# Grouped-query decode attention: a loop of two blocks run 15 times, with K in three 32 KB pieces

## The chip, the core and the metric

One core of a Trainium2 chip runs the whole kernel. The time is device microseconds of one execution, as the median of three runs; beside it one execution was profiled, and its trace is what the views below come from. The engines are PE (matrix multiply, with its weight loads shown as PEld), DVE (vector), ACT (scalar functions), POOL (GpSimd) and SP, which here only issues DMAs. Every large load is issued by SP and runs on 16 DMA engines.

## What is computed

A decode step of attention for one token, mixed with a small token mixer by a gate:

```python
q = (x @ wq)                       # 16 heads of 256
scores = einsum("bhqd,bhkd->bhqk", q, k) * (256 ** -0.5)   # k: 8 kv heads x 65536 keys x 256
p = softmax(scores)
a = einsum("bhqk,bhkd->bhqd", p, v).reshape(1, 1, 16 * 256) @ wo
h = layernorm(x); u = gelu(einsum("bsd,sf->bdf", h, w1) + b1); b = einsum("bdf,fs->bds", u, w2) + b2
g = sigmoid((x * gate_w).sum(-1))
out = g * a + (1 - g) * b
```

x has 448 elements; K and V are 268 MB each in bf16. Two query heads share one K/V head.

## The kernel before

The keys are cut into 32 blocks of 16,384: four per K/V head. A block's K and V are 8.39 MB each. Partition p of a tile holds 128 consecutive keys, so a full K or V block is 64 KB per partition, and half of it 32 KB.

SBUF holds one K block in two tiles of 32 KB per partition (`k_tiles[0]`, `k_tiles[1]`, shown as kn), one V block in one tile of 64 KB (`vt`), two tiles `kT` for transposed K, and the whole output projection `wo_sb` (28 KB per partition).

A block runs through `block` (L537), whose order is the order on each engine, since `seq` ties every instruction to the one before it on its engine:

- `score_block` (L381): eight steps; in each DVE transposes 16 keys per partition (L365) into one of the two kT tiles, and PE makes 8 matmuls into the score tile (L373). The first four steps read the first K tile, the last four the second.
- the loads, issued by SP: `load_v` of this block (L130), then the two halves of the next block's K (L124). V waits until the P·V of the block before has read vt; each K half waits for the four transposes that read its tile.
- `softmax` (L425): a maximum on DVE (L431), a transpose on PE (L435), the running maximum, the exponential on ACT (L452), a transpose of the weights on DVE (L460). Blocks after the first of a head rescale the running sums; the first one overwrites them. In a head's last block DVE copies the next head's q (`place_q`, L303).
- `products`: 64 matmuls of P·V (L393), then DVE adds them to the running sum (L470, L475).
- in a head's last block `denominators` and `head_end` (L508): normalise, collect, project with Wo (L503), add to `a_acc` (L514).

Ahead of that stand the q projection, the layer norm, and 14 gelu activations on ACT (L263) whose results lie in wo_sb until Wo is loaded. Block 0 is peeled off: it has the gate's sum, the mixer's 14 matmuls and tail as hooks between its steps, and issues the load of 14 heads of Wo (3.2 MB).

The loop (L556) runs 7 times over four blocks, with a `tc.stage_boundary()` between blocks; with `iteration_sync="staggered"` the loop body is cut into four stages, and each engine has semaphore instructions at each boundary and at the back edge. Three blocks follow it. The last block's V goes into the two K tiles in eight pieces, which P·V and `columns` take up one by one.

Of the kernel before, what the change touches and what calls it, by code (L numbers as in the profile page):

```python
# [14 lines left out]
HQ = 16  # L15
# [11 lines left out]
QW = 128 + 2 * NI  # L27


@with_exitstack  # L30
def kernel(
# [48 lines left out]
    kvpool.tile([128, 4096 - 128], mybir.dt.uint8, name="fill")  # L80
    k_tiles = [kvpool.tile([128, KP, DH], BF16, name=f"kn{i}") for i in range(2)]
# [4 lines left out]
    wo_sb = const.tile([128, HQ, 2, D], BF16)  # L86
# [5 lines left out]
    f_tiles = [psum.tile([64, MC], FP32, name=f"f{i}") for i in range(2)]  # L92
    f_rows = [f_tiles[k][32 * k:32 * k + 1, :] for k in range(2)]
# [13 lines left out]
    gel = wo_sb[:].rearrange("p h c n -> p (h c) n")[:, 0:NF, :]  # L107

    def place(n):
        return n if isinstance(n, tuple) else divmod(n, NB)  # L110

    def following(n):
        g, b = place(n)
        return (g + (b + 1) // NB, (b + 1) % NB)

    def rows(cache, n):
        g, b = place(n)
        return cache[0, bass.ds(g, 1), b * BLK:(b + 1) * BLK, :].rearrange(
            "o (p j) d -> (o p) j d", j=VP
        )  # L120

    def load_k(n, h, pieces=((0, KP),)):
        for j0, j1 in pieces:
            seq(nc.sync.dma_start(  # L124
                out=k_tiles[h][:, j0:j1, :],
                in_=rows(A_k_cache, n)[:, h * KP + j0:h * KP + j1, :],
            ))

    def load_v(n, j0=0, j1=VP):
        seq(nc.sync.dma_start(out=vt[:, j0:j1, :], in_=rows(A_v_cache, n)[:, j0:j1, :]))  # L130
# [3 lines left out]

    LAST = ((0, 32), (32, 64), (64, 80), (80, 96), (96, 112), (112, 120), (120, 124), (124, 128))

    def load_wo(h0, h1):
        seq(nc.sync.dma_start(
            out=wo_sb[:, h0:h1],
            in_=A_wo[h0 * DH:h1 * DH, :].rearrange("(h p c) n -> p h c n", p=128, c=2),  # L140
        ))

    def load_v_last(n):
        for j0, j1 in LAST:
            seq(nc.sync.dma_start(
                out=k_tiles[j0 // KP][:, j0 % KP:(j1 - 1) % KP + 1, :],
                in_=rows(A_v_cache, n)[:, j0:j1, :],
            ))
# [12 lines left out]
    load_k(0, 0, ((0, 32), (32, KP)))  # L161
    load_k(0, 1)
# [74 lines left out]
    xf = work.tile([128, D], FP32)  # L237
    h_bc = work.tile([128, D], FP32)
    w1f = const.tile([128, NF], FP32)
    b1f = const.tile([128, NF], FP32)  # L240
    seq(nc.vector.tensor_copy(out=xf[:], in_=sm_ps[:, 0:D]))
    seq(nc.vector.bn_stats(out=stats[:], in_=xf[:]))
# [8 lines left out]
    for _ in range(2):  # L251
# [7 lines left out]
        out=h_bc[:], in0=xf[:], scalar1=mv[:, 0:1], scalar2=rstd[:, 0:1],  # L259
        op0=ALU.subtract, op1=ALU.mult,  # L260
    ))
    for b in range(NF):
        seq(nc.scalar.activation(  # L263
            out=gel[:, b, :], in_=h_bc[:], func=ACT.Gelu_apprx_tanh,
            scale=w1f[:, b:b + 1], bias=b1f[:, b:b + 1],
        ))
# [30 lines left out]
    qq = const.tile([128, 2 * NW, HQ], BF16)  # L297
    seq(nc.vector.tensor_copy(out=qq[:], in_=qq_ps.rearrange("p (w h) -> p w h", h=HQ)))

    def place_q(g):  # L300
        for a in range(NQ):
            quad = slice(32 * a, 32 * (a + 1))
            seq(nc.vector.tensor_copy(  # L303
                out=qz[quad, :, 2 * NI + 32 * a:2 * NI + 32 * a + REP],
                in_=qq[quad, :, bass.ds(g * REP, REP)],
            ))

    place_q(0)
    zt = work.tile([1, D], FP32)
# [7 lines left out]
    def gate_sum():  # L317
        seq(nc.vector.tensor_tensor(out=zt[:], in0=xf[0:1, :], in1=gw[:], op=ALU.mult))
        seq(nc.vector.tensor_reduce(out=z[:], in_=zt[:], op=ALU.add, axis=AXIS.X))
        seq(nc.scalar.activation(out=ez[:], in_=z[:], func=ACT.Exp, scale=-1.0))  # L320

    def mixer_tail():
# [4 lines left out]
        y_ps = hd_ps[0:1, 0:D]  # L327
        for b in range(NF):
            seq(nc.tensor.matmul(
                y_ps, lhsT=w2b[:, b:b + 1], rhs=gel[:, b, :], start=(b == 0), stop=(b == NF - 1)  # L330
            ))
# [29 lines left out]
    def parity(n):  # L361
        return place(n)[1] % 2

    def transposes(i):
        seq(nc.vector.transpose(  # L365
            out=kT_tiles[i % 2][:].rearrange("p j w k c -> p (j w k c)").bitcast(FP32),
            in_=k_tiles[i // 4][:, i % 4 * NJ:(i % 4 + 1) * NJ, :].rearrange("p j d -> p (j d)").bitcast(FP32),
        ))

    def scores(n, i):  # L370
        for w in range(NW):
            for c in range(2):
                seq(nc.tensor.matmul(  # L373
                    sc_tiles[parity(n)][:, :],
# [6 lines left out]
    def score_block(n, hooks={}):  # L381
        for i in range(NI):
            transposes(i)
            scores(n, i)
            if i in hooks:
                hooks[i]()

    def pv(n, ip, jjs=range(NJ), tile=None, dst=pv_ps, last_ip=NI // 2 - 1):
        pT = pT_tiles[parity(n)]
# [12 lines left out]
    def pv_one(n, i):  # L402
        ip, e = divmod(i, 2)
        for jj in range(NJ):
# [3 lines left out]
                lhsT=pT_tiles[parity(n)][:, 32 * jj + 2 * REP * ip:32 * jj + 2 * REP * (ip + 1)],  # L408
# [5 lines left out]
    def columns(j0, j1):  # L414
        for j in range(j0, j1):
            i, jj = divmod(j, NJ)
            for c in range(2):
                seq(nc.tensor.matmul(
                    o_last[:, c, :],
                    lhsT=k_tiles[j // KP][:, j % KP, :].rearrange("p (d c) -> p c d", c=2)[:, c, :],  # L420
                    rhs=pT_tiles[parity(L)][:, 32 * jj + REP * i:32 * jj + REP * (i + 1)],
# [3 lines left out]
    def softmax(n, fill=None):  # L425
        g, b = place(n)
        fill = fill or [lambda: None] * 3
        sc_ps = sc_tiles[b % 2]
        nb, nb_old = nb_tiles[b % 2], nb_tiles[(b + 1) % 2]
        al, pT = al_tiles[b % 2], pT_tiles[b % 2]  # L430
        seq(nc.vector.tensor_reduce(out=rmax[:], in_=sc_ps[:, :], op=ALU.max, axis=AXIS.X))  # L431
        if b == NB - 1 and n != L:
            place_q(g + 1)
# [4 lines left out]
            out=(mrun if b == 0 else mnew)[:],  # L438
# [3 lines left out]
        if b > 0:  # L442
# [4 lines left out]
        fill[2]()  # L447
        seq(nc.vector.tensor_tensor_reduce(  # L448
# [7 lines left out]
        if b > 0:  # L456
            seq(nc.scalar.activation(
                out=al[:], in_=nb_old[:], func=ACT.Exp, scale=-1.0, bias=nb[:, 0:1]
            ))
        seq(nc.vector.transpose(out=pT[:, :], in_=p_sb[:, :]))  # L460
        if b > 0:
            seq(nc.vector.scalar_tensor_tensor(  # L462
                out=lsum[:], in0=lsum[:], scalar=al[:, 0:1], in1=den[:], op0=ALU.mult, op1=ALU.add
            ))
        else:
            seq(nc.vector.tensor_copy(out=lsum[:], in_=den[:]))

    def accumulate(n, src=pv_ps):
        if place(n)[1] > 0:
            seq(nc.vector.scalar_tensor_tensor(  # L470
                out=acc[:], in0=acc[:], scalar=al_tiles[parity(n)][:, 0:1], in1=src[:, :, :],
                op0=ALU.mult, op1=ALU.add,
            ))
        else:
            seq(nc.vector.tensor_copy(out=acc[:], in_=src[:, :, :]))  # L475

    def denominators():
# [6 lines left out]
            out=esc[:], in0=fst[:], scalar1=rden[:, 0:1], scalar2=None, op0=ALU.mult  # L484
# [14 lines left out]
    def project(g):  # L499
        a_ps = hd_ps[0:1, 0:D]  # L500
        for r in range(REP):
            for c in range(2):
                seq(nc.tensor.matmul(  # L503
                    a_ps, lhsT=oT[:, c, r:r + 1], rhs=wo_sb[:, bass.ds(g * REP + r, 1), c, :],
                    start=(r == 0 and c == 0), stop=(r == REP - 1 and c == 1),
                ))

    def head_end(g):  # L508
        collect(esc, True, True)
        for c in range(2):  # L510
            seq(nc.vector.tensor_copy(out=oT[:, c, :], in_=o_ps[c]))
        project(g)
        a_ps = hd_ps[0:1, 0:D]
        seq(nc.vector.tensor_tensor(out=a_acc[:], in0=a_acc[:], in1=a_ps, op=ALU.add))  # L514

    L = NBLK - 1

    def products(n):
        for ip in range(NI // 2):
            pv(n, ip)  # L520
        accumulate(n)
# [15 lines left out]
    def block(n, hooks={}, extra=None):  # L537
        g, b = place(n)
        score_block(n, hooks)
        load_v(n)  # L540
        load_k(following(n), 0)
        load_k(following(n), 1)
        if extra:
            extra()
        softmax(n)
        if b == NB - 1:
            denominators()
        products(n)
        if b == NB - 1:
            head_end(g)  # L550

    seq(nc.vector.memset(a_acc[:], 0.0))
    block(0, {2: gate_sum, 5: mixer_tail, 6: gate_column}, lambda: load_wo(0, HQ - REP))

    last.clear()
    with tc.For_i(0, HKV - 1, 1, iteration_sync="staggered") as g:  # L556
        for i in range(NB):
            if i > 0:
                tc.stage_boundary()
            block((g, i + 1) if i < NB - 1 else (g + 1, 0))  # L560
    last.clear()

    for n in range(NBLK - NB + 1, NBLK):
        if n < L - 1:
            block(n)
            continue
        if n < L:
            score_block(n)
        else:
            score_block(n, {1: result_base, 2: lambda: pv(L - 1, 0), 3: lambda: pv_one(L - 1, 2)})  # L570
        if n == L - 1:
            load_v(n, 0, 48)
            load_k(L, 0)
            load_k(L, 1)
            load_v(n, 48, VP)
        else:
            load_v_last(L)
            for h in range(HQ - REP, HQ):
                load_wo(h, h + 1)
        if n < L:  # L580
            softmax(n)
        else:
# [8 lines left out]
            softmax(n, [lambda: pv_one(L - 1, 3), lambda: pv(L - 1, 2, range(4)), rest_base])  # L591
# [4 lines left out]
            accumulate(L - 1)  # L596
# [8 lines left out]
    for ip in range(2):  # L605
        pv(L, ip, tile=k_tiles[0][:, 32 * ip:32 * (ip + 1), :], dst=pv_last, last_ip=1)
    accumulate(L, pv_last)
# [13 lines left out]
    for r in range(REP):  # L621
        for c in range(2):
            for k in range(2):
                seq(nc.tensor.matmul(  # L624
                    f_rows[k], lhsT=oT[:, c, r:r + 1],
                    rhs=wo_sb[:, HQ - REP + r, c, k * MC:(k + 1) * MC],
# [36 lines left out]
```

## Time and profile before

| what | us |
|---|---|
| median of 3 runs (1266.9 to 1267.49) | 1267.18 |
| the profiled execution | 1267.32 |
| its span, first to last instruction | 1265.5 |
| PE busy, of the span | 790.3 (62%) |
| DVE busy | 683.7 (54%) |
| ACT busy | 43.1 (3%) |
| score matmuls L373, 2048 | 550.4, 419 ns each |
| transposes L365, 256 | 571.3, 2283 ns each |
| P·V L393, 1968 | 178.6, 541 ns each |

The span is what lies between the first and the last instruction; the profiled execution's own time is 1.8 us longer. In a group's row the time after the bar is the engine's idle time just before these instructions, and what ended it. In a timeline row stand the start, the duration, engine, line, operation and the tiles; in brackets the idle time before it and its releaser. In a row of semaphore records stand the count, the shortest, median and longest duration in ns, and the first and last start. The granted clock of PE is a share of full speed; its mean is 0.798.

### The profile page before, as it was taken

How to read it: one execution, taken by the hardware profiler on the slowest of the kernel's cores; microseconds unless marked ns; L12 is line 12 of the kernel's file. 1: busy time of each engine (PE TensorE's matmuls, PEld its weight loads, DVE VectorE, ACT ScalarE, POOL GpSimd, SP SyncE). 2: the span in 40 equal slices, each digit the busy share in tenths (PEclk: the TensorE clock that was granted, in tenths of full speed). 3: DMA queues.
4: the chain of work that ended last, by engine and by line, in shares of the span. 5: the costliest groups of instructions: out<-in, count | busy, mean ns of one | idle time of the engine just before them, and what ended most of it. 6: DMA issues, size and time to landing. Idle time of an engine off the chain costs nothing.

```text
span 1265.5 us, 11451 instructions
## 1 busy us (share of the span) xinstructions
PE 790.3 (62%) x4577; PEld 308.4 (24%) x4577; DVE 683.7 (54%) x620; ACT 43.1 (3%) x108; POOL 1.7 (0%) x7
## 2 busy tenths in 40 slices
PE   4566567575666666575765566755757555676576
PEld 2222122222222222222222222222223222222123
DVE  5465455654446654456554466544566444665472
ACT  4000000000000000000000000000000000000000
POOL 0000000000000000000000000000000000000000
PEclk9687778787687877788877878677788778787787
DMA  9999999999999999999999999999999999999997
GB/s 413 415 444 433 429 423 437 434 438 431 426 438 435 445 431 433 419 438 435 439 433 426 433 437 446 433 433 419 436 435 441 431 428 431 437 446 432 417 442 334
DMA packets 17955, 544.40 MB, mean 430 GB/s; under 512 B 2197, under 2 KB 4248, under 8 KB 4760
## 3 DMA queue, kind: packets, MB, share of 16 engines
q1 hardware_dynamic: 17506, 544.22, 99.6%
q8 instruction: 10, 0.16, 0.0%
q10 hardware_dynamic: 438, 0.01, 0.0%
q14 instruction: 1, 0.01, 0.0%
HBM read 544.22 MB, written 0.00 MB: 430 GB/s over the span
## 4 chain that ended last, share of the span: by engine, by line
DMA 58%; PE 13%; issue 13%; DVE 11%; SPq 0%; DVEq 0%
DMA kn<-in_A_k_cache_dram 42%; DMA vt<-in_A_v_cache_dram 15%; DVE kT L365 10%; PE sc L373 9%; PE pv_ps L393 2%; DMA kn<-in_A_v_cache_dram 2%; PE hd_ps L503 1%; DVE acc L470 0%; PE hd_ps L492 0%; SPq L124 0%; PE sm_ps L492 0%; PE f L624 0%; DVEq L365 0%; SPq L556 0%; SPq L130 0%
## 5 line engine op out<-in xcount | busy, mean ns | idle before, releaser
L373 PE MATMUL sc<-kT,qz 128*128 128x512 bf16 x2048 | 550.4, 419 | 241.6 <-DVE kT L365 241.6
L365 DVE STREAM_TRANSPOSE kT<-kn 128x2048 f32<-128x2048 f32 x256 | 571.3, 2283 | 118.9 <-DMA kn<-in_A_k_cache_dram 69.5
L373 PEld LDWEIGHTS <-qz 128*128 128x128 bf16 x2048 | 212.4, 104 | 579.1 <-issue 380.9
L393 PE MATMUL pv_ps<-vt,pT 128*4 128x512 bf16 x1968 | 178.6, 541 | 146.8 <-DMA vt<-in_A_v_cache_dram 105.6
L470 DVE SCALAR_TENSOR_TENSOR acc<-acc,al,pv_ps 128x512 f32<-128x512 f32 x23 | 17.2, 747 | 206.4 <-PE pv_ps L393 139.1
L393 PEld LDWEIGHTS <-pT 128*4 128x4 bf16 x2000 | 58.8, 111 | 260.1 <-issue 208.5
L452 ACT ACTIVATE p_sb<-sc,nb 128x512 bf16<-128x512 f32 x32 | 22.0, 687 | 1186.8 <-DVE nb L448 1186.8
L431 DVE TENSOR_REDUCE rmax<-sc 128x1 f32<-128x512 f32 x32 | 22.1, 691 | 65.7 <-PE sc L373 51.4
L475 DVE COPY acc<-pv_ps 128x512 f32<-128x512 f32 x8 | 5.5, 692 | 72.9 <-PE pv_ps L393 72.9
L460 DVE STREAM_TRANSPOSE pT<-p_sb 128x512 bf16<-128x512 bf16 x32 | 22.8, 711 | 29.3 <-ACT p_sb L452 29.3
L435 PE MATMUL sm_ps<-ident_f,rmax 128*1 128x128 f32 x32 | 8.7, 273 | 24.7 <-DVE rmax L431 24.7
L444 PE MATMUL sm_ps<-mrun,ones_f 1*128 1x2 f32 x64 | 12.3, 260 | 17.1 <-DVE mrun L443 14.7
L444 PEld LDWEIGHTS sm_ps<-mrun,ones_f 1*128 1x128 f32 x64 | 9.6, 186 | 23.4 <-DVE mrun L443 19.4
L448 DVE CUSTOM_DVE_ANT_0 junk<-sm_ps,nval 128x2 f32<-128x2 f32 x32 | 5.1, 159 | 17.5 <-PE sm_ps L444 17.5
L478 PE MATMUL hd_ps<-lsum,same 128*128 128x1 f32 x14 | 3.7, 333 | 14.6 <-DVE lsum L462 14.6
L435 PEld LDWEIGHTS sm_ps<-ident_f,rmax 128*1 128x1 f32 x32 | 2.5, 79 | 40.6 <-DVE rmax L431 40.4
L503 PE MATMUL hd_ps<-wo_sb,oT 128*1 x28 | 9.9, 448 | 0.4
L263 ACT ACTIVATE wo_sb<-h_bc,b1f,w1f 128x448 bf16<-128x448 f32 x14 | 9.2, 748 | 7.4 <-DVE h_bc L258 7.4
L437 DVE TENSOR_REDUCE mnew<-sm_ps 1x2 f32<-1x64 f32 x24 | 5.1, 212 | 7.2 <-PE sm_ps L435 7.0
L514 DVE TENSOR_TENSOR a_acc<-a_acc,hd_ps 1x448 f32<-1x448 f32 x7 | 4.3, 608 | 8.6 <-PE hd_ps L503 8.6
L492 PE MATMUL hd_ps<-esc,acc 128*128 128x2 f32 x28 | 4.4, 263 | 7.0 <-DVE acc L470 7.0
L274 PE MATMUL hd_ps<-xm,vt 128*128 128x1 bf16 x96 | 3.7, 165 | 5.2 <-DMA vt<-in_A_wq_dram 5.2
(103 smaller groups left out, 111.0 us busy)
## 6 DMA issues: line engine op xcount, KB each, us to landing
kn<-in_A_k_cache_dram SPq DMA_DIRECT2D x63, 4096.0 KB, 28.4
vt<-in_A_v_cache_dram SPq DMA_DIRECT2D x1, 5120.0 KB
kn<-in_A_k_cache_dram SPq DMA_DIRECT2D x2, 2048.0 KB, 12.2
kn<-in_A_v_cache_dram SPq DMA_DIRECT2D x2, 2048.0 KB, 22.3
wo_sb<-in_A_wo_dram SPq DMA_DIRECT2D x1, 3136.0 KB
vt<-in_A_wq_dram SPq DMA_DIRECT2D x1, 3072.0 KB, 10.1
vt<-in_A_v_cache_dram SPq DMA_DIRECT2D x1, 3072.0 KB
kn<-in_A_v_cache_dram SPq DMA_DIRECT2D x3, 1024.0 KB, 21.7
```

What stands on the lines that cost most here:

```text
L263: seq(nc.scalar.activation(out=gel[:, b, :], in_=h_bc[:], func=ACT.Gelu_apprx_tanh, scale=w1f[:, b:b + 1], bias=b1f[:, b:b + 1],))
L365: seq(nc.vector.transpose(out=kT_tiles[i % 2][:].rearrange("p j w k c -> p (j w k c)").bitcast(FP32), in_=k_tiles[i // 4][:, i % 4 * NJ:(i ...
L373: seq(nc.tensor.matmul(sc_tiles[parity(n)][:, :], lhsT=qz[:, 2 * w + c, 2 * (NI - i):2 * (NI - i) + 128], rhs=kT_tiles[i % 2][:, :, w, :, ...
L393: seq(nc.tensor.matmul(dst[32 * grp:32 * grp + 2 * REP, :, :], lhsT=pT[:, 32 * jj + 2 * REP * ip:32 * jj + 2 * REP * (ip + 1)], rhs=pairs( ...
L431: seq(nc.vector.tensor_reduce(out=rmax[:], in_=sc_ps[:, :], op=ALU.max, axis=AXIS.X))
L435: seq(nc.tensor.transpose(sm_ps[0:1, 0:128], rmax[:, 0:1], ident_f[:, :]))
L444: seq(nc.tensor.matmul(sm_ps[:, 128:128 + REP], lhsT=ones_f[0:1, :], rhs=mrun[0:1, :], start=True, stop=True))
L452: seq(nc.scalar.activation(out=p_sb[:, :], in_=sc_ps[:, :], func=ACT.Exp, scale=scale, bias=nb[:, 0:1], accum_out=den[:, 0:1],))
L460: seq(nc.vector.transpose(out=pT[:, :], in_=p_sb[:, :]))
L470: seq(nc.vector.scalar_tensor_tensor(out=acc[:], in0=acc[:], scalar=al_tiles[parity(n)][:, 0:1], in1=src[:, :, :], op0=ALU.mult, op1=ALU.a ...
L475: seq(nc.vector.tensor_copy(out=acc[:], in_=src[:, :, :]))
L503: seq(nc.tensor.matmul(a_ps, lhsT=oT[:, c, r:r + 1], rhs=wo_sb[:, bass.ds(g * REP + r, 1), c, :], start=(r == 0 and c == 0), stop=(r == RE ...
```

## The change

The loop becomes two blocks, run 15 times, for blocks 0 to 29; blocks 30 and 31 follow it. Block 0 is no longer peeled off. Every block of the loop now rescales, and two columns `caps` that change sign after each odd block (`turn`) make the rescaling an overwrite in the first block of a head. `ends` does the same for the projection: every odd block does a `head_end`, and in those which are not a head's last its weights are zero. `place_q` runs in every odd block, from a table `qq` that holds each head's q twice.

Wo shrinks to two heads per partition; one head is loaded in each turn of the loop and moved from slot 1 to slot 0 by ACT after the projection. The gelu results, xf, h_bc and zt lie in the third K piece until the loop starts. The mixer's matmuls and the gate's sum come ahead of the loop, its tail in block 30.

K has three pieces of 32 KB per partition: `k_low`, and the two halves of `k_high`. Even blocks read the first half of k_high and then k_low, filled by two transfers; odd blocks read both halves of k_high, filled by one transfer with 64 KB rows. The last block's V goes into k_low and the second half of k_high.

Each block of the loop has two stages: its scores and the issue of its V, then a new `tc.stage_boundary()`, then the issue of the next K, softmax and products. The core of the diff:

```diff
-    k_tiles = [kvpool.tile([128, KP, DH], BF16, name=f"kn{i}") for i in range(2)]
+    k_low = kvpool.tile([128, KP, DH], BF16, name="k_low")
+    k_high = kvpool.tile([128, 2 * KP, DH], BF16, name="k_high")
+    slots = [k_low[:], k_high[:, 0:KP, :], k_high[:, KP:, :]]
...
-    wo_sb = const.tile([128, HQ, 2, D], BF16)
+    wo_sb = kvpool.tile([128, REP, 2, D], BF16, name="wo_sb")
...
+    def load_k_whole(n):
+        seq(nc.sync.dma_start(out=k_high[:], in_=rows("k", n)))
...
+    def turn():
+        seq(nc.vector.tensor_scalar(
+            out=caps[:], in0=caps[:], scalar1=-1.0, scalar2=None, op0=ALU.mult
+        ))
+        seq(nc.vector.tensor_scalar(
+            out=ends[:], in0=ends[:], scalar1=-1.0, scalar2=1.0, op0=ALU.mult, op1=ALU.add
+        ))
...
+        if may_begin:
+            seq(nc.vector.tensor_tensor(
+                out=nbo[:], in0=nb_old[:], in1=caps[:, 0:1], op=ALU.max
+            ))
+            nb_old = nbo
...
+        seq(nc.scalar.copy(out=wo_sb[:, 0], in_=wo_sb[:, 1]))
...
-    block(0, {2: gate_sum, 5: mixer_tail, 6: gate_column}, lambda: load_wo(0, HQ - REP))
+    gate_sum()
+    mixer_sum()
...
-    with tc.For_i(0, HKV - 1, 1, iteration_sync="staggered") as g:
-        for i in range(NB):
-            if i > 0:
+    with tc.For_i(0, HQ - 1, 1, iteration_sync="staggered") as t:
+        for e in range(2):
+            if e:
                 tc.stage_boundary()
-            block((g, i + 1) if i < NB - 1 else (g + 1, 0))
+            score_block(e, (1, 2) if e else (1, 0))
+            load_v(2 * t + e)
+            tc.stage_boundary()
+            if e == 0:
+                load_k_whole(2 * t + 1)
+                load_wo(t, 1)
+                softmax(e, may_begin=True)
+                products(e)
+            else:
+                load_k(2 * t + 2, 0, 1)
+                load_k(2 * t + 2, 1, 0)
+                softmax(e, pair=t + 1)
+                denominators()
+                products(e)
+                head_end()
+                turn()
...
-    for n in range(NBLK - NB + 1, NBLK):
+    for n in (L - 1, L):
```

In the changed program SP's order in a turn is V of the even block, boundary, whole K of the odd block, a head of Wo, boundary, V of the odd block, boundary, the two halves of the next even block's K.

## Prediction

> **What bounds the kernel now.** I read the page first, then the DMA rate by stretch, then one block's instructions in order of time, then the semaphore records at a stage boundary. The page's queue table and DMA strip:
>
> ```profile
> DMA  9999999999999999999999999999999999999997
> ...
> q1 hardware_dynamic: 17506, 544.22, 99.6%
> ```
>
> SP's queue keeps the 16 DMA engines busy for 99.6% of the span, so 544.2 MB set the time. The windows table (last three columns: clock granted to TensorE, DMA share, GB/s), over one block's period of 38.68 us:
>
> ```profile
> 420.00:458.68 38.68, 23.45 (x131) 8.85 (x131) 20.56 (x17) 0.96 (x3) 0.00 (x0) 0.76 1.00 434
> ```
>
> Share 1.00: 16.78 MB in 38.68 us. An 8.39 MB V or K therefore takes 19.3 us, a 229 KB head of Wo 0.55 (0.53 at that rate, a little more for its 1.8 KB rows). PE and DVE have 15 us to spare per block. The chain of waits (DMA 58%) agrees. So the question is not what an instruction costs, but whether the queue ever runs dry. DVE's and SP's timelines of one block:
>
> ```profile
> 456.68 4.50 DVE L365 STREAM_TRANSPOSE kT<-kn 128x2048 f32<-128x2048 f32 x2 [2.75 <-DMA kn<-in_A_k_cache_dram]
> 462.36 13.28 DVE L365 STREAM_TRANSPOSE kT<-kn 128x2048 f32<-128x2048 f32 x6 [1.18 <-PE sc L373]
> 477.63 0.69 DVE L431 TENSOR_REDUCE rmax<-sc 128x1 f32<-128x512 f32 x1 [1.99 <-PE sc L373]
> ```
> ```profile
> 467.01 9.10 SPq L124 DMA_DIRECT2D kn<-in_A_k_cache_dram  x2
> 494.82 0.33 SPq L130 DMA_DIRECT2D vt<-in_A_v_cache_dram  x1
> ```
>
> The first half of K lands at 456.7; SP issues the next K's first half at 467.0, when the fourth transpose frees the tile, with V (landing at 485.8, when P·V starts) still streaming. Nothing runs dry.
>
> **What a stage boundary is.** Semaphore records of the loop's line around one boundary:
>
> ```profile
> L556 SPq EVENT_SEMAPHORE  x4: 17/17/17, 105.1 to 105.3; - x4
> L556 PEldq EVENT_SEMAPHORE  x3: 51/51/51, 102.8 to 105.2; - x3
> L556 DVEq EVENT_SEMAPHORE  x3: 21/21/21, 105.0 to 105.2; - x3
> ```
>
> PE's sequencer arrives at 102.8 and goes on only at 105.1, after DVE's at 105.0; ACT, GpSimd and SP go on then too. SP issues V at 105.55. After a head's end the timeline has the last P·V at 491.1, DVE's last sum starting at 494.29, V's issue at 494.82: not when vt is free but 0.5 us after the last engine arrives. **A boundary is a rendezvous of all five sequencers.** Before, all boundaries stand between blocks. After, each block has one more, between its scores and its next K loads.
>
> **Part by part.** Times run from T0, the first transpose of an odd block.
>
> 1. *Merged K, loads behind the new boundary (the term that decides).* The next K needs every sequencer past the block's score matmuls. DVE's is there at T0 + 17.5. PE's is seen by the record that follows its last score matmul, here the block with T0 = 224.82:
>
> ```profile
> L435 PEldq EVENT_SEMAPHORE  x1: 51/51/51, 244.9 to 244.9; - x1
> ```
>
> That is T0 + 20.1 (the sequencer runs 1.5 us ahead of the array: that block's last score matmul starts at T0 + 21.6). Two more blocks give 19.7 and 19.6; over all blocks of the loop the last matmul starts at T0 + 20.95 on average, so I take **19.45**. Then 0.5 us to SP's issue (above). From issue to bytes on an idle queue, only the first DMA shows it: issue at 0.74, and
>
> ```profile
> 1.00:1.50 0.50, 0.00 (x0) 0.00 (x0) 0.00 (x0) 0.00 (x0) 0.50 (x1) 1.00 0.00 0
> 1.50:2.00 0.50, 0.00 (x0) 0.00 (x0) 0.00 (x0) 0.00 (x0) 0.47 (x2) 1.00 3.35 739
> ```
>
> so between 0.8 and 1.3; I take 1.2, for the slowest of 16 engines. Next K's bytes start at T0 + 21.15. What is queued behind the odd block's K: Wo 0.55 and V 19.3, ending 19.85 us after K's last byte, which came about 0.3 us ahead of T0 (bounds 0 and 0.4: V's last packets end 0.4 us ahead of the P·V they release): T0 + 19.55. **The queue is dry for 1.6 us** in each of 15 odd blocks: +24. Before, K's first half came 9.7 us sooner, and with it the scores; one 64 KB-row transfer lands whole and takes that lead away. Bounds of one gap: 0.8 (scores end 20.4, DMA start 0.8) to 2.8 (PE not ahead of its array by the 1.5 us).
>
> 2. *Even blocks.* From the first byte of their K: the odd block before ends at 14.5 (softmax 4.7 after its scores, P·V 5.9, head end 3.0 by the 491.26 to 494.29 rows, two small DVE operations 0.3), scores reach the boundary near 34.7, the merged K starts at 36.4. V streams until 38.7. **No gap, with 2.3 us of cover**; without the cover, each us lost costs 15.
>
> 3. *The peeled first block goes.* Before, V(0) is issued at 15.67, behind K(0), and nothing runs dry. After, SP waits at loop entry for K(0) to land. DVE's timeline:
>
> ```profile
> 32.72 2.31 DVE L365 STREAM_TRANSPOSE kT<-kn 128x2048 f32<-128x2048 f32 x1 [2.73 <-DMA kn<-in_A_k_cache_dram]
> ```
>
> K(0) lands at 32.6, its bytes end at 32.3. Loop entry takes SP 1.1 (DVE's sum starts at 67.32, barrier 67.7, V issued 68.86), the queue 1.2: V's bytes at 34.9. **+2.6.** The first V issue in the loop also took 3.03 us against 0.33 later; I think it waited behind the 3 MB Wo load, which is gone; if not, 3 more. gel and ez are done at 27 (gel ends at 25.53, table load 1.28, ez 0.20), so the other engines enter at about 28 and block 0's scores end at 47.5, under V(0).
>
> 4. *Bytes and packets.* In the trace's DMA packets 32 KB takes 1213 ns, 64 KB 2418: 8 ns per pair, 8 pairs per engine, 15 blocks: **-1**. Wo is loaded 15 + 2 times, one head more than 16: **+0.5**. In each loop turn Wo follows K, and is in term 1.
>
> 5. *New small instructions* (caps, ends, nbo, one ACT copy of Wo, 0.1 to 1 us each) lie in softmax and head end, counted in 2. *Exit:* block 29's head end and a barrier put V(30)'s issue at 3 us ahead of need, and block 30 starts 5.5 us late, 8 with the mixer's tail. V(31) no longer waits for block 31's transposes; PE's last columns come out level with the last V piece: **0**, at most +3.
>
> The DMA page of the Trainium skill ("DMA: Bandwidth & Descriptors", Rules for kernel authors) advises to coalesce many small transfers into one large; its fit of 2.0 us fixed per DMA (same page, GpSimd path) would make 15 fewer DMAs worth an estimated 30 us, about 1237. No run here shows a fixed cost between queued transfers.
>
> **Sum.** 1265.5 + 24 + 2.6 - 1 + 0.5 = 1291.6 span. Around it lie 1.8 us (1267.32 for the profiled execution), which is 0.1 above the median: **1293.3**.
>
> **Rivals.** (a) *A second gap*, in even blocks: P·V at a low granted clock (6.4 instead of 5.9, both ends seen in the loop) and a slow score block (21.6) use up 1.2 of the 2.3 us; a slower loop turn does the rest, and 1 us per turn adds 15: 1308. For: every link is serial. Against: the rows leave a rest. 15%. (b) *The gap closes*: PE's sequencer passes by T0 + 17.9, near DVE's 17.5, so the queue never dries; only terms 3 and 4 stay: 1269.4. Against: the records at 19.6 to 20.1. 7%. (c) *Faster*: queued transfers hide a pause that merging removes, which decides if it exceeds the gap. Room for it is the 0.4% of the span in which no packet ran, 5.1 us, of which 1.8 lies ahead of the first packet: at best 1263. Against: share 1.00 over whole blocks. 3%. The coalescing rule of the Trainium skill's DMA page points to (c). (d) That the merged load is cut in two again would change term 4 alone.
>
> **How the numbers follow.** Forecast 75%, (a) 15%, (b) 7%, (c) 3%. One gap of 0.8 to 2.8 us spans 1281 to 1311, and takes in most of (a); left out are (b), (c) and the far end of (a). This kernel's measurement tells 0.2% (2.5 us) from no change: faster 3%, same 6%, slower 91%.
>
> **What would show it.** The DMA strip shows 9s still, but the windows over a two-block period of some 79.4 us (77.4 before) give a share near 0.98; each odd block has a stretch of about 1.6 us without bytes just before its next K, and none in even blocks. K issues of odd blocks stand at T0 + 20, where before they stood at T0 + 10.3. The first V is issued near 33.7. Wrong would be: K issued ahead of the last score matmuls, a share of 1.00, or a second dry stretch per turn.

## Result and profile after

The changed kernel takes **1302.73 us** (median of 5 runs, 1301.9 to 1303.08) against 1266.9 for the kernel before (5 runs on the same chip, 1266.74 to 1267.49): a ratio of 1.0281, 95% interval 1.027 to 1.0292. It is 2.8% slower. The profiled execution's own time is 1302.78, its span 1301.0, which is 35.5 us more than before; the granted clock averaged 0.807 (0.798 before), so the clock is not the cause.

The page of the changed kernel, DMA strip and queue table:

```profile
DMA  9989999999999999999999999999999999999998
...
q1 hardware_dynamic: 15698, 544.45, 97.7%
```

SP's queue still moves the same bytes, but its packets now fill 97.7% of a longer span, where 99.6% stood before. The windows over three loop turns, each from about the first transpose of one odd block to that of the next odd block (columns: stretch, length, busy time of PE, PEld, DVE, ACT and POOL, granted clock, DMA share, GB/s):

```profile
232.50:312.72 80.22, 47.04 (x276) 18.88 (x276) 43.61 (x45) 2.86 (x7) 0.00 (x0) 0.84 0.99 425
312.72:392.94 80.22, 50.86 (x276) 19.75 (x276) 43.30 (x44) 2.86 (x7) 0.00 (x0) 0.78 0.96 413
393.08:473.30 80.22, 48.35 (x276) 19.25 (x276) 43.58 (x45) 2.86 (x7) 0.00 (x0) 0.82 0.98 421
```

A turn of two blocks takes 80.22 us (two blocks took 77.36 before), with a share of 0.96 to 0.99. To see where in the turn the share goes, take one odd block. DVE's timeline gives its start, T0 = 312.45, and the end of its scores:

```profile
312.45 4.50 DVE L388 STREAM_TRANSPOSE kT<-k_high 128x2048 f32<-128x2048 f32 x2 [13.39 <-DMA k_high<-in_A_k_cache_dram]
...
334.08 0.69 DVE L453 TENSOR_REDUCE rmax<-sc 128x1 f32<-128x512 f32 x1 [1.99 <-PE sc L396]
```

SP's timeline around it:

```profile
298.72 0.33 SPq L135 DMA_DIRECT2D vt<-in_A_v_cache_dram  x1
332.53 0.33 SPq L126 DMA_DIRECT2D k_high<-in_A_k_cache_dram  x1
...
348.99 0.33 SPq L135 DMA_DIRECT2D vt<-in_A_v_cache_dram  x1
369.73 0.33 SPq L132 DMA_DIRECT2D k_high<-in_A_k_cache_dram  x1
```

The block's V was issued while the block before it was at work. SP issues nothing between 298.72 and 332.53, and the next K is issued at T0 + 20.08. What SP waited for stands in the semaphore records at the loop's line:

```profile
L564 DVEq EVENT_SEMAPHORE  x3: 21/21/21, 329.7 to 332.3; - x3
L564 PEldq EVENT_SEMAPHORE  x3: 51/51/51, 332.2 to 332.5; - x3
L564 SPq EVENT_SEMAPHORE  x2: 17/17/17, 332.2 to 332.3; - x2
```

DVE's sequencer reaches the boundary at 329.7, PE's only at 332.2, and SP goes on at 332.2: PE is the last, and it is the one that holds the load back. The windows of half a microsecond around it (the same columns):

```profile
331.50:332.00 0.50, 0.36 (x2) 0.08 (x1) 0.50 (x1) 0.00 (x0) 0.00 (x0) 1.00 0.02 0
332.00:332.50 0.50, 0.35 (x2) 0.19 (x2) 0.09 (x1) 0.00 (x0) 0.00 (x0) 1.00 0.00 0
332.50:333.00 0.50, 0.50 (x4) 0.19 (x2) 0.00 (x0) 0.00 (x0) 0.00 (x0) 1.00 0.00 0
333.00:333.50 0.50, 0.50 (x4) 0.24 (x3) 0.00 (x0) 0.00 (x0) 0.00 (x0) 1.00 0.22 66
333.50:334.00 0.50, 0.50 (x3) 0.05 (x1) 0.00 (x0) 0.00 (x0) 0.00 (x0) 1.00 3.05 852
```

(A packet counts where it starts, so a share can exceed 1.) The V that was queued ends at 331.96, the new K's first packet starts at 333.50, 0.97 us after its issue. For 1.54 us the DMA engines have nothing to do, and PE is busy with the scores they are waiting for. Fifteen such stretches, of 0.84 to 1.60 us (1.16 on average), lie in the trace, one in each odd block; in the even blocks there is none: K issued at 369.73 joins a V that still streams.

### The profile page after: what moved, and what is told of

It is laid out like the page before. It is cut to its first block, busy times and chain, and to the rows that moved or that the text cites. A ratio compares the mean times of both kernels' runs of the same rounds, so it can differ in the third digit from the quotient of the medians.

```text
span 1301.0 us, 12083 instructions
## 1 busy us (share of the span) xinstructions
PE 797.8 (61%) x4689; PEld 318.6 (24%) x4689; DVE 708.1 (54%) x754; ACT 58.6 (5%) x131; POOL 1.7 (0%) x7
## 3 DMA queue, kind: packets, MB, share of 16 engines
q1 hardware_dynamic: 15698, 544.45, 97.7%
## 4 chain that ended last, share of the span: by engine, by line
DMA 55%; issue 39%; PE 2%; SPq 1%; DVE 1%; ACT 0%; DVEq 0%
DMA wo_sb<-in_A_wo_dram 26%; DMA k_low<-in_A_k_cache_dram 23%; DMA vt<-in_A_v_cache_dram 3%; DMA k_high<-in_A_k_cache_dram 2%; DMA k_high<-in_A_v_cache_dram 2%; PE sc L396 1%; DVE kT L388 1%; SPq L126 1%; SPq L132 0%; PE pv_ps L416 0%; SPq L564 0%; PE f L644 0%; SPq L144 0%; PE hd_ps L532 0%; ACT p_sb L484 0%
## 5 line engine op out<-in xcount | busy, mean ns | idle before, releaser
L388 DVE STREAM_TRANSPOSE kT<-k_high 128x2048 f32<-128x2048 f32 x192 | 431.2, 2288 | 251.4 <-DMA k_high<-in_A_k_cache_dram 193.4
L416 PE MATMUL pv_ps<-vt,pT 128*4 128x512 bf16 x1968 | 164.8, 508 | 30.3 <-DVE pT L491 14.5
L388 DVE STREAM_TRANSPOSE kT<-k_low 128x2048 f32<-128x2048 f32 x64 | 141.6, 2270 | 0.0
L497 DVE SCALAR_TENSOR_TENSOR acc<-acc,al,pv_ps 128x512 f32<-128x512 f32 x31 | 23.2, 748 | 159.1 <-PE pv_ps L416 159.1
L537 ACT COPY wo_sb<-wo_sb 128x896 bf16<-128x896 bf16 x15 | 14.1, 937 | 143.2 <-PE hd_ps L532 143.2
L532 PE MATMUL hd_ps<-wo_sb,oT 128*1 128x448 bf16 x60 | 19.3, 420 | 0.0
L518 PE MATMUL hd_ps<-esc,acc 128*128 128x2 f32 x60 | 9.5, 263 | 14.0 <-DVE acc L497 14.0
L536 DVE TENSOR_TENSOR a_acc<-a_acc,hd_ps 1x448 f32<-1x448 f32 x15 | 9.1, 608 | 15.9 <-PE hd_ps L532 15.9
L518 PEld LDWEIGHTS hd_ps<-esc,acc 128*128 128x128 f32 x60 | 8.2, 196 | 21.6 <-DVE acc L497 21.6
L503 PEld LDWEIGHTS hd_ps<-lsum,same 128*128 128x128 f32 x30 | 5.9, 245 | 30.1 <-DVE lsum L492 30.1
```

What stands on the lines that cost most here:

```text
L388: seq(nc.vector.transpose(out=kT_tiles[i % 2][:].rearrange("p j w k c -> p (j w k c)").bitcast(FP32), in_=slots[pair[i // 4]][:, i % 4 * N ...
L416: seq(nc.tensor.matmul(dst[32 * grp:32 * grp + 2 * REP, :, :], lhsT=pT[:, 32 * jj + 2 * REP * ip:32 * jj + 2 * REP * (ip + 1)], rhs=pairs( ...
L497: seq(nc.vector.scalar_tensor_tensor(out=acc[:], in0=acc[:], scalar=al_tiles[e][:, 0:1], in1=src[:, :, :], op0=ALU.mult, op1=ALU.add,))
L503: seq(nc.tensor.matmul(hd_ps[:, 460:461], lhsT=same[:].rearrange("p a r -> p (a r)"), rhs=lsum[:, 0:1], start=True, stop=True,))
L518: seq(nc.tensor.matmul(o_ps[c], lhsT=acc[:, e, :].rearrange("p (d c) -> p c d", c=2)[:, c, :], rhs=weights[:, e, :], start=(start and e == ...
L532: seq(nc.tensor.matmul(a_ps, lhsT=oT[:, c, r:r + 1], rhs=wo_sb[:, r, c, :], start=(r == 0 and c == 0), stop=(r == REP - 1 and c == 1),))
```

## Experiments

**Theory.** It takes both parts together. The merged transfer makes the odd block's scores late, and the new boundary ties the next K's issue to the end of those scores. **Rivals:** the boundary alone is at fault (a rendezvous costs by itself); the merged transfer alone is; the head of Wo that lies in the queue between K and V. Each ratio below is to the kernel before on the same chip, which took 1267.16 us in both groups (e1 to e4: 15 runs; e5 to e7: 12).

### e1: the boundary without the merged transfer

```diff
-                load_k_whole(2 * t + 1)
+                load_k(2 * t + 1, 0, 1)
+                load_k(2 * t + 1, 1, 2)
```

> Edit: the odd block's K comes again in two transfers of 32 KB rows (into the two halves of k_high); everything else, the new stage boundary between scores and K loads too, stays as changed. Theory (the queue runs dry because the merged K lands whole, so that the scores and with them the boundary come 9.7 us later than the first half alone would let them): scores reach the boundary 9.7 us sooner against the queue, no dry stretch is left, the 36 us of 15 gaps (2.4 each in the trace of the changed kernel) go: 1266.7 plus 1 us for the packets, 1267 to 1269. Rival A (a boundary in the middle of a block costs by itself, five sequencers meeting 60 times instead of 28): the time stays above 1290.

Measured: 1266.72 us (10 runs), ratio 0.9998 (0.9989 to 1.0007): the expected range missed by 0.3 us at its lower end. DVE's timeline of one odd block (T0 = 217.66), and SP's:

```profile
217.66 4.50 DVE L388 STREAM_TRANSPOSE kT<-k_high 128x2048 f32<-128x2048 f32 x2 [2.95 <-DMA k_high<-in_A_k_cache_dram]
223.30 13.28 DVE L388 STREAM_TRANSPOSE kT<-k_high 128x2048 f32<-128x2048 f32 x6 [1.14 <-PE sc L396]
238.57 0.69 DVE L453 TENSOR_REDUCE rmax<-sc 128x1 f32<-128x512 f32 x1 [1.99 <-PE sc L396]
```
```profile
237.02 0.33 SPq L126 DMA_DIRECT2D k_high<-in_A_k_cache_dram  x1
255.95 0.33 SPq L135 DMA_DIRECT2D vt<-in_A_v_cache_dram  x1
```

The boundary still holds K's issue back to T0 + 19.4. But T0 itself is the landing of the first half, so the second half, Wo and V are still to come, and the new K's first packet waits until 245.4 behind them. The whole loss is gone: the boundary, the two-block loop, Wo by heads and the small added instructions cost nothing that can be measured.

### e2: the merged transfer without the boundary

The loop body is four blocks, run seven times, with boundaries between blocks only; blocks 28 and 29 follow it.

```diff
+    def block(n, t, e):
+        score_block(e, (1, 2) if e else (1, 0))
+        load_v(n)
+        if e == 0:
+            load_k_whole(n + 1)
...
+    with tc.For_i(0, HKV - 1, 1, iteration_sync="staggered") as g:
+        for i in range(NB):
+            if i:
+                tc.stage_boundary()
+            block(4 * g + i, 2 * g + i // 2, i % 2)
```

> Edit: the merged K stays, the loop body is four blocks run 7 times with boundaries between blocks only, blocks 28 and 29 unrolled behind it; SP issues the next K right behind V, when the fourth transpose has freed the piece. Theory (the merged transfer starves nothing by itself; the boundary between scores and loads does, with it): K's issue goes back to 10 to 12 us behind an odd block's first transpose, no dry stretch, 1265.5 to 1268.5. Rival B (one transfer that lands whole is itself what costs, wherever its issue stands): above 1290.

### e3 and e4: the boundary earlier in the block

The loads and the boundary move from behind the scores to behind step 4 (e3) or step 6 (e4) of the eight.

```diff
-            score_block(e, (1, 2) if e else (1, 0))
-            load_v(2 * t + e)
-            tc.stage_boundary()
+            def loads(e=e):
+                load_v(2 * t + e)
+                tc.stage_boundary()
...
+            score_block(e, (1, 2) if e else (1, 0), {4: loads})
```

> Edit: the two-block loop and the merged K stay; V's issue, the boundary and the next K's issue move from behind the eighth score step to behind the fifth (hook 4). Theory (PE's sequencer must have sent the last score matmul ahead of the boundary): it now needs only the fifth step's, some 6.6 us sooner, so K is issued near 13.5 us behind the first transpose, 14.5 for the first bytes, 5 us before the queue would run dry at 19.6: no gap, 1265.5 to 1268, level with the kernel before. Rivals A and B both keep it above 1290.

> Edit: as the boundary behind the fifth step, but behind the seventh (hook 6), one step of 2.2 us sooner than in the changed kernel. Theory: K issued 2.2 us sooner, near 17.7; first bytes near 18.8, the queue dry at 19.6: the gap of 1.6 us closes with 0.7 us to spare in a usual turn and stays open a little in turns with a slow PE clock. 1266 to 1272, so one step of eight is worth nearly all of the 36 us. If the loss went on with the distance of the boundary from the loads instead (a price per us of delay, no threshold), it would be near 1302.7 less 3/8 of what the fifth step gains, about 1291.

Measured: e2 1275.9 us (4 runs), ratio 1.007 (1.0054 to 1.0085); e3 1275.26 (5 runs), 1.0066 (1.0053 to 1.008); e4 1279.37 (4 runs), 1.0099 (1.0084 to 1.0115). Of the 35.8 us of loss, three quarters go in e2 and e3 and two thirds in e4. All of it was expected to go, or nearly all, so all three expectations missed: each result is over 7 us above the top of its range. A second loss must lie in e2 and e3. The page of e2, and then rows of its SP and DVE timelines (this odd block's T0 is 227.80):

```profile
q1 hardware_dynamic: 15698, 544.45, 99.4%
```
```profile
238.41 0.33 SPq L126 DMA_DIRECT2D k_high<-in_A_k_cache_dram  x1
...
263.19 0.33 SPq L135 DMA_DIRECT2D vt<-in_A_v_cache_dram  x1
```
```profile
259.17 0.75 DVE L497 SCALAR_TENSOR_TENSOR acc<-acc,al,pv_ps 128x512 f32<-128x512 f32 x1 [4.91 <-PE pv_ps L416]
...
262.65 0.61 DVE L536 TENSOR_TENSOR a_acc<-a_acc,hd_ps 1x448 f32<-1x448 f32 x1 [1.37 <-PE hd_ps L532]
```

K is issued at T0 + 10.6 and is in time. The V of the next even block is issued at T0 + 35.4, behind the odd block's head end: P·V is done by 259.17, DVE's last sum of that head starts at 262.65, and the boundary between blocks comes after it. The first DMA engine runs out of K at 264.98, the last at 266.65. V came 1.8 us before the first of them was free, and this was too late. Two sums over the trace's packets, from 30 to 1250 us, show the loss: the time in which engines had no packet (idle), and the time above the usual 1.21 us (32 KB) or 2.42 us (64 KB) that slowed packets took (slowed, counting those at least 5% over). Both are in us, as a mean of the 16 engines:

| kernel | idle | slowed | of both, around the new K | of both, around the next V |
|---|---|---|---|---|
| before | 0.7 | 0.2 | 0.1 | 0.2 |
| after | 25.8 | 9.5 | 34.1 | 0.2 |
| e2 | 2.3 | 5.8 | 0.1 | 7.3 |
| e3 | 1.5 | 5.4 | 0.2 | 5.6 |
| e4 | 5.6 | 6.8 | 10.8 | 0.9 |

So e2 and e3 lose around V, not around K. In e4 it is K again: issued at 245.51, T0 + 17.5, it comes 1.4 us ahead of the first free engine (246.95), which is no more enough than the 1.8 us were. I had expected little or nothing left of the gap from that point on, and that was wrong.

### e5: V's issue ahead of the head end

e2 with one step moved: the next block's V is issued right behind the last P·V, ahead of the sum and the head end.

```diff
+            for ip in range(NI // 2):
+                pv(e, ip)
+            if next_v:
+                load_v(n + 1)
+            accumulate(e)
+            head_end()
+            turn()
```

> Edit, on the four-block loop (1275.9): the next block's V is issued right behind P·V, ahead of the running sum and the head end, so that no boundary stands between P·V and it. Theory (second wait: with merged K the odd block ends 9.7 us later, and V for the next block, issued 35.8 us behind the odd block's first transpose, comes as the queue's last K packets end at 37 to 39; the engines that are ahead run dry): V is issued near 32, some 4 us sooner, no engine runs dry, 1265.5 to 1267.5. Rival B (64 KB rows of K cost by themselves): stays at 1274 to 1277.

### e6: no head end in the loop

e3 without one line.

```diff
-                head_end()
```

> Edit, on the two-block loop with the boundary behind the fifth step (1275.3): the head end is left out of the loop, so the kernel leaves out collecting and projecting heads 0 to 14. Theory (second wait, as above): the odd block ends 3.2 us sooner, V with it, no dry engine, 1265.5 to 1268. Rival B: 1274 to 1277.

Measured: e5 1267.07 us (10 runs), ratio 0.9999 (0.999 to 1.0009). e6 1266.18 (one run). SP's timeline of e5 (T0 = 227.59) and of e6 (T0 = 227.42):

```profile
237.88 0.33 SPq L126 DMA_DIRECT2D k_high<-in_A_k_cache_dram  x1
...
258.65 0.33 SPq L135 DMA_DIRECT2D vt<-in_A_v_cache_dram  x1
```
```profile
259.69 0.33 SPq L135 DMA_DIRECT2D vt<-in_A_v_cache_dram  x1
```

Both lie in their expected ranges. V is issued at T0 + 31.1 and T0 + 32.3, and the first engine is free for it at 264.25 and 264.32: 5.6 and 4.6 us of lead in these blocks, and the slowed packets are gone (0.3 and 0.1 us in all). Both ways of taking the head end out from between P·V and V's issue remove the second loss. e5 keeps the merged transfer, all 15 of them, and takes the time of the kernel before. The windows over the same 1080 us, kernel by kernel, show three rates; the changed kernel:

```profile
100.00:1180.00 1080.00, 667.62 (x3735) 262.55 (x3731) 587.36 (x594) 39.06 (x95) 0.00 (x0) 0.80 0.98 422
```

e2:

```profile
100.00:1180.00 1080.00, 667.38 (x3794) 262.77 (x3787) 595.15 (x599) 39.05 (x95) 0.00 (x0) 0.81 1.00 431
```

e5:

```profile
100.00:1180.00 1080.00, 687.47 (x3835) 268.37 (x3824) 603.93 (x603) 39.06 (x95) 0.00 (x0) 0.80 1.00 434
```

e1 and the kernel before have 434 too. Note e2's row: the share says 1.00 and yet 0.7% of the rate is missing. A packet that takes longer counts as busy; only GB/s shows it.

### e7: no Wo in the queue

```diff
                 load_k_whole(2 * t + 1)
-                load_wo(t, 1)
```

> Edit, on the changed kernel (1302.7): the loop's loads of Wo are left out, so the projection of heads 0 to 14 uses zeros. 15 times 229 KB less is 8.4 us of transfer. Theory (what lies in the queue between K and the next K's issue is cover, one for one): each gap grows by the 0.56 us that the load no longer covers, and nothing is won: 1301 to 1304. Rival (the queue's bytes still set the time, and gaps are a fixed price): 1293 to 1296.

Measured: 1304.72 us (4 runs), ratio 1.029 (1.0271 to 1.0308). The page of e7:

```profile
q1 hardware_dynamic: 13538, 541.01, 97.1%
```

It moves 3.44 MB less, 7.9 us at 434 GB/s, and saves nothing. Engines stand idle for 34.2 us (25.8 in the changed kernel), 8.4 more. What lies in the queue between K and the next K is cover, one for one, and the rival that Wo costs its 8 us falls. The time came out 0.7 us above the range that was expected.

No version here beats the kernel before measurably: with the queue never dry, e1 and e5 come back to it, and its 434 GB/s were the highest rate over those 1080 us in any of these kernels.

## Why the prediction came out right, and where it was off

The direction, the mechanism and its place were right, and 1302.73 lies in the range; the forecast of 1293.3 was 9.4 us too low. By its own steps:

1. **The gap in odd blocks.** Place and size right, its consequence mis-sized: this is **the term that failed**. I had the queue dry at T0 + 19.55 and bytes again at T0 + 21.15; in the block above they are 331.96 - 312.45 = 19.51 and 21.05. That block is one of the longer ones: over the fifteen, K is issued at T0 + 19.7 on average, and no engine has a packet for 1.16 us. But the engines don't all stop and start at once: the first has its packet of the new K 0.97 us after the issue, the last 1.4 to 2.0, where I had taken 1.2 for the slowest. By engine, idle around the new K sums to 25.4 us, or 1.7 a block; 24 was forecast. So that size is right in part because an issue taken 0.2 us too late and a last engine taken too early partly cancel. What I left out is that the stream doesn't come back at full rate. The first K packet of each engine behind a dry stretch took 1.73 to 1.88 us on average, stretch by stretch, and the second 1.21 again: some 0.6 us in each of 15 turns, 8.8 us in all. The packets of e1, e5 and before show that it isn't the transfer: there the same 32 KB packets start behind other work and take 1.21. e7, with its longer dry stretches, has 1.65 to 1.84 again, so the price is about the same for a stretch of 1 us and one of 1.8. And the trace of before held the row: its very first packets, 24 KB on an idle queue, took 1.6 to 2.1 us where later ones of that size took 0.91. I read the 0.8 to 1.3 us up to the first byte from that same place and stopped there. A gap should have been priced at 1.6 + 0.6. With the 2.6 us of term 3, which did not come (see 3), that gives 1302, without them 1300.
2. **Even blocks.** Right: no gap, rival (a) falls. Why the second loss of e2 and e3 doesn't show here: K's bytes come 3 us later in the changed kernel (T0 + 21.05, in e2 245.61 - 227.80 = 17.8), so V, issued at T0 + 36.5, still finds over 4 us of K ahead of it. It is not gone but covered by the first loss, and it comes out when the first is mended.
3. **The peeled first block.** Wrong, +2.6 forecast. SP doesn't wait for K(0) at loop entry. The rows of ACT and SP there:

```profile
27.12 0.20 ACT L329 ACTIVATE ez<-z 1x1 f32<-1x1 f32 x1
27.46 0.35 SPq L135 DMA_DIRECT2D vt<-in_A_v_cache_dram  x1
```

V(0) is issued right behind ez, with K(0) still streaming, and no dry stretch follows. I had taken the entry of the loop for a wait on the tile's landing; by these rows it is a wait for the engines, and those were done at 27, as the prediction said of all but SP. The first issue takes 0.35 us, not 3.03.
4. **Bytes and packets.** Right within the rounding: 64 KB packets took 2.42 us, twice a 32 KB packet of 1.21.
5. **Small instructions and exit.** Right, and on the better side: the DMA stream ends 35.5 us later than before, at 1297.4 against 1261.9, so the tail behind it is unchanged.

The sum of 35.5 us of span: 24.3 of idle beyond that of before, over the whole span; 9.0 from 32 KB packets (1247 ns on average instead of 1213, 264 per engine); 1.6 from 64 KB packets (2423 instead of 2419, 360 per engine); Wo +0.5, fewer packets -1.0. That is 34.4; 1.1 us I have not placed. Against the forecast this is 10.6 more for slowed packets, 0.3 for idle time and the 1.1, less the 2.6 of term 3. So the error in term 3 hid a part of the error in term 1, and the forecast is nearer than its terms: that part is luck.

Rival (b), that PE passes its boundary early enough, fell by the records at 332.2. Rival (c), that merging is faster, fell for the merging itself: against e1, e2 is slower by 9 us and e5 the same (1266.72 and 1267.07, with 15 transfers between them). The coalescing rule of the Trainium skill ("DMA: Bandwidth & Descriptors", Rules for kernel authors) is for many small transfers, above all those under 64 KB; between queued transfers of 4 MB merging won nothing here: share 1.00 and 434 GB/s with them merged or not. Rival (d) was e1, and it was more than term 4: cutting the transfer in two takes the whole loss away.

How much lead a transfer needs can be read from the packets of all nine traces, between 80 and 1190 us. Lead is the time from SP's issue until the first engine is through with the transfer ahead; a loss is idle and slowed time around the start. The 28 transfers issued 0 to 1.5 us ahead lost 0.16 to 1.2 us each. Of the 19 issued 1.5 to 2.5 us ahead some lost nothing and some up to 1.0 us. None of those issued 2.5 us ahead or more lost over 0.15 us, and nearly all lost nothing. A lead of 0.97 us can't do for all 16 engines, since on a dry queue the last one has its first packet only 1.4 to 2.0 us after the issue. Why packets are slowed at some starts with 1.5 to 2.5 us of lead and not at others stays open, and so does the reason for the slow restart.

## What to carry to other kernels

Before merging transfers of a stream that binds, ask what the earlier landing of the first part was good for: here it started the scores 9.7 us sooner, and those released the next load. A boundary that costs nothing and a merge that costs 0.7% (through V's late issue, as e5 shows) cost 2.8% together, since each had used up the other's cover; try such parts alone and in pairs. Price a dry queue as the wait plus a slow restart, and look for the loss in GB/s, not only in the busy share.

## What the runs showed of the hardware

- A queue that has run dry pays twice: 0.97 us from issue to the first packet (332.53 to 333.50) and 1.4 to 2.0 until the last engine has one, and first packets of 32 KB that take about 1.8 us instead of 1.21 on each engine. The Trainium skill ("DMA: Bandwidth & Descriptors", Specifications) gives about 0.6 us to the first byte for such a DMA; the trace has 0.97 from the start of SP's issue, and 0.64 from the end of that instruction, which takes 0.33.
- The 16 DMA engines don't end a transfer together: in e2 the first is through K at 264.98 and the last at 266.65. So a transfer that is late for the first engine already loses, with the queue's share still at 1.00.
- First packets are slowed even where hardly an engine stood idle: e2 has 2.3 us of idle time and 5.8 us in slowed packets, its V's first 64 KB packets taking 2.5 to 3.0 us on average instead of 2.42.
